# Four more sets of four d_ff blocks by seven block products, in a sparse attention and squared-relu kernel on one core

## The chip, the core and the metric

The kernel runs on one core of one Trainium2 chip. Times are device microseconds of that core. The engines are TensorE (PE in the profile, with its weight loads as PEld), VectorE (DVE), ScalarE (ACT), GpSimd (POOL) and SyncE (SP). POOL and SP issue the transfers between memory and the core's buffers; SP also issues the transposes that are made by a transfer.

## What is computed

The reference is attention with 4 batches of 768 tokens, 8 heads of 64 channels, where a token sees 8 global tokens and the last 96, with a bias that grows with distance; its output, 3072 tokens by 512 channels, goes through two weight matrices with a squared relu between.

```
scores = scale * np.matmul(q, k.transpose(0, 1, 3, 2))
...
keep = is_global | is_local
...
a = np.exp(scores)
a = a / (np.sum(a, axis=-1, keepdims=True) + 1e-09)
...
x = np.ascontiguousarray(attn_out.transpose(0, 2, 1, 3)).reshape(B * S, H * D)
h = np.maximum(x @ w_in, 0.0)            # 3072 x 512 by 512 x 2048
return (h * h @ w_out).astype(np.float32)  # 3072 x 2048 by 2048 x 512
```

## The kernel before

**Halves.** The 3072 tokens are cut into eight halves of a batch (`halves[0]` to `halves[7]`, 384 tokens each). Each half goes through attention (scores, exp on ScalarE, a product with a mask on VectorE, the product with the values, a norm on VectorE), a transpose of the result to `x.xt` (channels on the partitions), layer 1 (`x.xt` by `w_in_sb`, relu, square, to `x.h2`) and layer 2 (`x.h2` by `w_out_sb`, to `y`, stored to memory). While layer 1 of one half runs, the scores and values of the next half and layer 2 of the half before are placed between its products.

**Layer 1 in two ways.** d_ff has 16 blocks of 128 hidden units. `layer1` makes one block plainly: four matmuls of 384 columns into a PSUM bank, then `relu` into `hr` on ScalarE or VectorE (L744, L746), and for each two blocks one `square` (L758, L760). The other way, `layer1_group`, takes four blocks at once: two near ones (2g and 2g + 1) and the two that lie eight blocks further, so that tokens, channels and hidden units form a 2 by 2 by 2 block product. It makes that product of eight block products by seven, as in Winograd's form of Strassen's method: the steps p1 to p7 are four matmuls of 192 columns each (L841), some with plain operands, some with sums of blocks. The sums of `x.xt` stand in `x_mix` (four sums per half, `list_x_mix`, L818). The sums of the weights stand in `in_mix` for the groups 1, 2 and 3 (`list_in_mix`, L785), and for group 0 in columns of `w_in_sb` whose plain weights aren't read any more (`list_late_mix`, L801).

**What a set of seven leaves to the other engines.** A bank of partial sums is copied out by `hold` (the tile `kept`, L256 on ScalarE, L258 on VectorE) three times, and the kept copies are added to later sums by `add`, an operation of VectorE alone (L901), which also takes the relu. In half 2 the sets are *seeded* (`SEEDS`): there one of the three adds is replaced by a copy of `kept` back into a bank (`seed`) and a plain `relu` (L907). Then come two squares (L924, L926).

**Which sets.** The strings of `LAYER1` say which groups of a half go by seven and in which sequence the steps are listed: the seven letters of a group's alphabet in `LETTERS` are its steps, an `s` is one plain block. In the kernel before, half 2 has groups 3 and 2 by seven and eight plain blocks, halves 3 and 4 have groups 3, 2 and 1 by seven and four plain blocks, halves 5, 6 and 7 have all four groups by seven: 20 sets. Halves 0 and 1 are plain.

**The order.** Every operation is first listed, by the stages above, in three lists: the jobs of TensorE (`p` and a number), the loads (`l`), and all the rest. The string `ORDER` then says in which sequence they are issued and on which engine: `a` ScalarE, `d` VectorE, `s` SyncE, `g` GpSimd; the digits behind a point are the PSUM banks that a job opens, `@` names a transfer that a load has to come behind. Each engine works its own words in that sequence. The numbers are places in the lists, so they shift when operations are added ahead of them.

Of the kernel before, what the change touches and what calls it, by code (L numbers as in the profile page):

```python
# [9 lines left out]
FP16 = mybir.dt.float16  # L10
# [3 lines left out]
P = 128  # L14
# [29 lines left out]
LAYER1 = {2: "sasbcsdABCsesDEsFGfsgs", 3: "as123456b7cdsAeBCfgDsEFsG",  # L44
          4: "AasBbCscDEdefF123ss45gG67", 5: "1A2BCDh3E45iF6jabckdlefgGm7n",
# [6 lines left out]
ORDER = """a4 d1 g2 p0.0 a6 s8 d12 a0 s10 d13 l3 l1 a18 l2 d15 d19 a26 d16 d3 l5 a30 d14 a20 a27 d9 l4 a23  # L52
d5 a22 d17 p1.12+31 a21 l0 p5.34 d11 a7 p10.56 l6 a28 p3 a24 l10 a31 d32 l9 a33 p6 d34 p4.7 a39
l7 p11 d37 a29 p9.0 p8.1 a46 l8 p2.23 d43 a40 p19.7 d35 l11 a47 p7 d55 a25 p13.51 d36 l13 a41
d44 p14.4 p12.67 d48 p15 a42 l12 d59 p17 a49 p16.0 p22.2 d45 l14 p24.4 a52 d51 p23.36 a50 d38
p34.50 l16 d58 a53 p21.7 d64 p25.2 a60 l18 p27.1 d65 a57 p20.4 a61 p32.37 d66 a81 d56 p31.2 l15
a73 p29.6 d68 p18.5 d72 p28.4 a74 p26.3 l19 p36.1 d54 a69 p35.2 p30.7 a86 d70 p33.54 d85 a71 d91
p39.16 a67 p40.27 a77 d63 p37.3 a82 d75 l17 a78 d62 p41.5 a92 d79 d76 p38.0 d84 d80 p45.4 d83
l21 a97 p48.1 d96 a101 l20 a98 p44.2 a89 p47.5 d107 l23 p46.7 a112 p42.0 d111 a108 d110 a93
p43.2 d109 p53.1 a87 p52.5 d102 p50.4 p49.7 a113 l22 d120 d100 a90 d105 p59.6 l27 a116 d119 a103  # L60
d106 p55.3 p51.1 l29 d94 a122 a88 d128 p65.2 l28 a104 d95 a117 p64.4 a118 p58.5 a129 a136 d114
p60.0 d99 a137 l30 d146 d191 p54.3 l24 p62.6 d115 d205 l25 p57.1 a133 p56.4 d125 d121 p63.7
p67.6 a123 d134 d135 a130 d206 p61.1 p72.3 a126 d132 p69.4 d189 a124 p77.7 a131 d156 p70.0 a142
p82.1 d157 d165 a159 p71.5 a160 p74.4 d162 l34 a166 d201 a163 p83.6 d147 a161 l26 p73.0 a167
d522 d164 a138 p84.3 l31 d158 d148 a168 a169 p79.52 d186 l35 a139 d202 p89.04 p81.1 d127 a198
l33 d151 p85 a187 d170 a178 d523 p86 a174 d207 a199 d184 p78.06 a179 d149 l32 p80.57 p88.41 d180
p87 a195 l36 d200 a175 p76.2 d203 a185 l37 d155 p75.4 a196 d193 p91.0 l38 a188 d143 s194 d197
p66.1 a181 l39 d172 a171 p95.3 d152 a173 p90.5 d223 p100.4 d153 a209 s224 a176 d236 p92 d204
p103.2 d177 d208 p68.3 d237 s216 a244 a140 d210 p93.6 d240 a211 p94 a182 d150 s217 a144 d219
p96.1 p104 d225 p97 d183 a245 d221 p98.7 s220 d239 a218 p102.3 d238 p111 d214 d228 s226 l44 p106  # L70
d222 d243 l43 d213 p109.61 s229 d227 p110.73 d154 p99 l40@217 a255 d258 s215 d141 p101 a256
l42@217 d145 a251 d272 d190 p113 l45 a252 a234 p114.73 d254 l41@217 d192 p108.61 p105.0 a248 l46
d246 a261 p107 d253 d259 a262 l47 d257 s260 p115.62 a249 s235 d230 p116.74 l48 p118.3 a264 d250
p131.1 a265 d232 d263 p117.6 a268 d231 a292 p122.2 d266 a273 p121.7 d233 a269 d212 p125.1 a271
d280 s324 p124 d284 p127.4 a283 p126 d241 a278 d267 p123.6 d285 a293 p137.1 s325 d281 p119.5
a287 p132 a286 p129.7 a279 d294 p130 p140 d323 a301 p142 d270 p134.6 a290 d274 a307 p128.1 a291
p135 d288 p133.2 a308 p136 d298 p141.5 a310 d300 s242 a299 p143.1 s282 a297 d309 p139 d326 p138
d524 p112 d395 l50@325 a305 s275 d311 p120 a303 l56 d306 a312 s289 d295 a302 p146.36 l53 p147.54
d304 p145.71 a330 s296 d313 l51@325 a333 p144.2 a331 d318 l52 p148.3 a334 d319 a276 l49@325
p149.5 d321 a327 a322 d433 d332 a328 l54 p151.64 p150.07 d314 p152 d320 a338 l57 d329 p159.1  # L80
a339 l55 p157.0 d336 a337 p172.7 a341 d340 p153 a352 d370 a342 p160.3 a350 d315 p169.6 s371 d353
a344 p158.7 p162 d351 p161 p154.4 d316 a355 d397 p166.3 a347 p164.7 d356 p163 s398 p156 d317
d358 d359 a366 p171.1 d343 p165 s399 p167 a360 d362 p181.7 a363 d335 a361 p170 d345 p175 d367
p177 a357 p174.0 d375 p173.5 a378 d373 p178.3 s247 s277 d369 p176 a383 s354 p180 d368 a372
p155.0 d349 a379 p168.1 a376 d382 a384 d400 p179 p183 l58@399 a364 p182.7 d380 a348 p184 s374
a377 l65 d385 p185.3 a389 l62 a387 d381 s386 p188.41 a365 d388 p187.05 l59@399 p186.27 a405
p189.6 d401 a409 l63 a413 d402 p190.0 a406 d416 l73 a410 d403 p191 a407 l61 d396 a414 p193.42
d412 a417 p194.65 l60@399 d411 a418 p192.71 p195 a422 d415 a419 l64 d391 p200.4 d429 a420 p206.7
d437 a426 p198.0 d392 p219.1 s438 d393 a434 d408 a427 p207.6 p204.4 d394 a447 s346 d489 p210
d443 a462 p202.5 a451 d428 p199.1 a423 d404 p211 a441 p213 d435 p197.4 p217.2 a432 d456 p205.5  # L90
s436 p218.1 d424 a444 d452 p196 d480 s491 a445 d476 a461 d460 p203.6 p215.7 d442 p223 a458 p221
d425 a453 p208 d421 s492 p209 d481 p220 a448 d483 p222.1 a469 d477 p214 a446 d467 p227.6 s390
d431 s468 p212.0 d457 p201 d449 a464 d493 a463 p216.1 d454 p224 a484 l70 p225 d459 s455 p230
a439 d473 a471 l66 d465 p226 a496 p231.50 d470 a474 l69@492 s430 p236.13 d478 p233.42 a497 s490
p228.7 d472 a503 l72 d482 a498 p229.5 l67@492 a509 d479 d494 a504 p241.4 l71 p235 a510 d485 d475
a527 d505 p237.01 a495 l68@492 a466 p232.72 d499 p234 l74 a500 d525 d486 a450 p245.3 d506 l75
p240.7 d508 p247 a512 s507 d515 p246.5 a533 p239 d488 a532 d487 d516 a526 p255 a501 p250 d520
p259.0 d544 s521 p249.2 d531 p243.6 d536 p252 a535 p238.3 d529 a540 d517 a513 p253 a549 d502
p261.5 s576 a519 p256 d514 p257.6 p270 d545 p263 d546 p244 a551 s440 a553 d541 a565 p248.1 d511
a530 p268.6 p272 d561 p267 a534 p251.2 d560 p260.4 a566 s562 p262 d537 p269 d550 p258.6 a542  # L100
p266 s547 d548 p242.4 a563 d538 a568 p254.0 a552 s577 d518 p264 a528 p271 a578 d554 p274 d567
d543 p265.7 p273 d579 p275 a580 a555 d569 p279 d558 a564 p281.2 d556 a596 a570 p276.60 a559 d585
s557 d571 p277.54 p278.71 a586 p280 d600 a593 s539 a589 d601 p282.6 a604 d603 a587 p286 a594
d598 d602 a590 p284.75 a605 d588 p283.03 p285.14 a609 p289 d595 a616 a613 s599 d668 p291 s574
a606 d619 d581 a607 p288.7 d572 p290.1 d622 a610 s575 d582 p303.0 a620 d591 p306.3 a639 d612
s573 p294 d608 a618 a643 d611 p323.5 a614 d671 d626 p305.4 p307 d642 p310 a644 p292.6 d584 d621
p295 a623 p321.4 d583 a628 d647 p296 d664 p312 d615 p298 s665 a629 p301 d650 p287.1 d632 p308.3
a617 s627 p297.4 d636 s597 p322 d645 p313.2 a666 d592 p299.6 a651 d631 p314 a648 p293.0 d652
p311.4 d624 p300 p316 d649 p315 a635 s625 p318.0 a633 d669 p302.4 d672 p309 a634 d655 p320 a667
p304 d653 p326 a662 d637 p324.2 d658 s638 a679 p325.7 a663 d646 s659 d640 p317 a678 p319 p335.4  # L110
d670 a654 p343.0 p328 d673 a707 a641 p334.6 d682 p327 d677 a698 d699 a656 p346.2 d674 a660
p349.3 d712 p337.1 a657 p351 d701 p342 a715 p338.2 d683 a661 p341.1 d680 p355 d675 s681 p329.7
d702 a717 s630 a705 d721 a706 p340 d687 p359 p348 d690 p345 d684 p350.2 d728 p339.3 d714 a704
p330 d688 a716 a703 p347 a691 d722 p354 p344 d710 p332 a720 d676 d708 p360 p362 d685 p331.1 a711
d713 a733 d689 p357 d709 p361 p353.3 a694 d686 a731 p366.0 d719 a692 a729 s693 d725 p352.4 a695
p333 a730 d732 p358 d696 p356 a734 d718 p336 d723 a697 d743 a726 p365.5 d746 a727 p363 d747 d744
p377.6 d700 a724 p364 d739 d735 p367.4 d740 a737 s736 d742 s738 d741 p368 a749 d745 d754 p371.3
d758 p373.2 d761 a762 d757 p369 a765 d750 d755 p374.1 d759 d756 d769 p376 d751 p375 d748 d760
p370 s752 a767 d768 a766 p380 d753 p378 d773 p379 d770 s774 p372 d771 s772 p381 a763 p382 d775
# [85 lines left out]
def kernel(  # L205
# [1312 lines left out]
    for hb in range(1, NHB):  # L1518
# [18 lines left out]
        if hb == 1 and GROUPS:  # L1537
            side.append((8 * 0.65, list_in_mix))
# [68 lines left out]
```

## Time and profile before

| | |
|---|---|
| median of 3 runs | 200.19 us (199.85 to 201.06) |
| the profiled execution | 200.43 us |
| its span, first to last instruction | 198.7 us |
| PE busy | 191.6 us, 96% |
| DVE busy | 176.3 us, 89%, 450 instructions |
| ACT busy | 151.0 us, 76%, 321 instructions |
| POOL busy | 66.9 us, 34% |
| granted TensorE clock | 1.000 of full speed |

The profile is of one execution, whose own time is 200.43 us: 1.73 us lie outside the span. An engine is busy from the start to the end of each of its instructions, and instructions that overlap count once. A "group" of the profile is all instructions of one line, engine and kind, with the mean duration of one of them; "idle before" is the idle time of that engine just ahead of them. The chain that ended last is followed back from the last instruction to what released each.

### The profile page before, as it was taken

The page shows a single profiled execution, that of the slowest core. Times are in us where ns is not written, and L with a number is a line of the kernel's source. Part 1 is how long each engine was busy: PE and PEld are TensorE (multiplying, and loading weights), DVE is VectorE, ACT ScalarE, POOL GpSimd, SP SyncE. Part 2 cuts the span into 40 slices and gives each one's busy share as a digit, 9 for nine tenths or more (in the row PEclk, how much of TensorE's full clock was granted, in tenths as well). Part 3 has the DMA queues.
Part 4 walks back from the last instruction along what each step waited for, and adds up shares of the span by engine and source line. Part 5 has one row for each costly group of instructions (what it writes and reads, how often), then busy time and mean ns, then how long its engine had stood idle before and what let it go on. Part 6 is the DMA issues. An engine that isn't in the chain of part 4 may idle for free.

```text
span 198.7 us, 5980 instructions
## 1 busy us (share of the span) xinstructions
PE 191.6 (96%) x2381; PEld 163.2 (82%) x2381; DVE 176.3 (89%) x450; ACT 151.0 (76%) x321; POOL 66.9 (34%) x82
## 2 busy tenths in 40 slices
PE   7798999999999999999999999999999999999993
PEld 3576899856888687788888998999889999999993
DVE  7589696899999999999989999899899996978971
ACT  6799797899555888976999679878897578769211
POOL 8996565187108701940194007800000000000000
PEclk9999999999999999999999999999999999999999
DMA  5999999999999998999899799996531221201214
GB/s 152 182 150 194 189 180 172 209 195 155 182 192 92 155 205 218 107 127 145 218 118 153 104 222 129 161 175 147 102 102 37 94 57 40 109 0 53 109 53 158
DMA packets 106987, 27.52 MB, mean 139 GB/s; under 512 B 97104, under 2 KB 104016, under 8 KB 106960
## 3 DMA queue, kind: packets, MB, share of 16 engines
q0 software_dynamic: 74944, 13.11, 90.1%
q1 hardware_dynamic: 30816, 13.45, 31.7%
q10 hardware_dynamic: 1200, 0.59, 1.1%
q8 instruction: 18, 0.29, 0.6%
q14 instruction: 9, 0.07, 0.1%
HBM read 27.26 MB, written 6.29 MB: 169 GB/s over the span
## 4 chain that ended last, share of the span: by engine, by line
PE 78%; DMA 7%; POOL 5%; DVE 5%; ACT 3%; issue 1%; POOLq 0%; DVEq 0%
PE yps L1064 32%; PE hps L841 19%; PE hps L717 14%; PE sp L610 4%; DMA xt<-tm 4%; DMA w_mix<-in_k_dram 4%; PE av L671 3%; PE yps L978 3%; POOL w_mix L396 2%; POOL v L396 1%; DVE hr L901 1%; ACT h L758 1%; PE av L1380 1%; PE trp L549 1%; DVE vb L258 1%
## 5 line engine op out<-in xcount | busy, mean ns | idle before, releaser
L623 ACT ACTIVATE ex<-sp 128x512 f16<-128x512 f32 x66 | 36.7, 632 | 3.6 <-PE sp L610 3.5
L1064 PEld LDWEIGHTS <-h 128*128 128x128 f16 x376 | 33.9, 98 | 4.0
L717 PE MATMUL hps<-xt,w_in_sb 128*128 128x128 f16 (+2 forms) x288 | 35.6, 273 | 0.3 <-ACT ex L1350 0.3
L256 ACT COPY kept<-hps 128x384 f32<-128x384 f32 x52 | 24.6, 490 | 12.4 <-PE hps L841 8.8
L901 DVE CUSTOM_DVE_ANT_0 hr<-hps,kept 128x384 f16<-128x384 f32 x58 | 30.3, 548 | 1.0 <-PE hps L841 0.6
L717 PEld LDWEIGHTS <-w_in_sb 128*128 128x128 f16 x288 | 23.5, 98 | 5.9 <-DMA w_in_sb<-in_moe_w_in_dram 0.5
L1064 PEld LDWEIGHTS <-mixed 128*128 128x128 f16 x272 | 25.2, 98 | 3.6 <-DVE mixed L1029 0.2
L396 POOL DMA_DIRECT2D sq<-in_q_dram x19 | 17.3, 910 | 31.0 <-DMA q<-sq 23.4
L256 ACT COPY y<-yps 128x256 f32<-128x256 f32 (+2 forms) x39 | 14.6, 385 | 15.8 <-PE yps L1064 15.8
L396 POOL DMA_DIRECT2D sk<-in_k_dram x19 | 17.1, 903 | 24.9 <-DMA q<-sq 22.4
L841 PEld LDWEIGHTS <-w_in_sb 128*128 128x128 f16 x288 | 24.4, 98 | 1.0
L841 PEld LDWEIGHTS <-in_mix 128*128 128x128 f16 x272 | 22.8, 98 | 1.1 <-issue 0.3
L841 PE MATMUL hps<-x_mix,in_mix 128*128 128x192 f16 x204 | 23.4, 246 | 0.0
L1064 PE MATMUL yps<-w_mix,h 128*128 128x256 f16 (+1 forms) x192 | 22.4, 264 | 0.0
L1064 PE MATMUL yps<-w_mix,mixed 128*128 128x256 f16 (+1 forms) x184 | 22.2, 268 | 0.0
L396 POOL DMA_DIRECT2D v<-in_v_dram x24 | 21.8, 922 | 1.2 <-DVE h L760 0.6
L1064 PE MATMUL yps<-w_out_sb,h 128*128 128x256 f16 (+1 forms) x184 | 21.9, 268 | 0.0
L924 ACT ACTIVATE h<-hr 128x768 f16<-128x768 f16 x25 | 20.9, 857 | 0.0
L647 DVE TENSOR_TENSOR phat<-ex,mask 128x1024 f16<-128x1024 f16 (+1 forms) x36 | 20.6, 590 | 0.1
L744 ACT ACTIVATE hr<-hps 128x384 f16<-128x384 f32 (+1 forms) x35 | 18.5, 546 | 2.8 <-PE hps L717 2.8
L841 PE MATMUL hps<-xt,w_in_sb 128*128 128x192 f16 x172 | 19.8, 246 | 0.0
L1126 DVE TENSOR_TENSOR y<-yps,y 128x256 f32<-128x256 f32 (+1 forms) x30 | 11.9, 408 | 3.5 <-PE yps L1064 2.9
(110 smaller groups left out, 354.1 us busy)
## 6 DMA issues: line engine op xcount, KB each, us to landing
out_dram<-y SPq DMA_DIRECT2D x23, 256.0 KB, 2.6
v<-in_v_dram POOLq DMA_DIRECT2D x24, 128.0 KB, 7.1
sq<-in_q_dram POOLq DMA_DIRECT2D x19, 128.0 KB, 6.4
sk<-in_k_dram POOLq DMA_DIRECT2D x19, 128.0 KB, 6.4
w_in_sb<-in_moe_w_in_dram POOLq DMA_DIRECT2D x4, 512.0 KB, 11.0
w_out_sb<-in_moe_w_out_dram POOLq DMA_DIRECT2D x4, 512.0 KB, 12.3
y<-in_q_dram SPq DMA_DIRECT2D x2, 256.0 KB, 4.4
y<-in_k_dram ACTq DMA_DIRECT2D x2, 256.0 KB, 5.1
```

The lines of the kernel that those rows point to most:

```text
L256: nc.scalar.copy(out=out, in_=in_)
L396: dma = nc.gpsimd.dma_start(out=dst, in_=src[x.b, :, r0 + t * P:r0 + (t + 1) * P, :] .rearrange("h p d -> p h d"))
L610: nc.tensor.matmul(sp[h][:, i, :], lhsT=lhsT, rhs=x.q[rows, r % HT, a, :], start=True, stop=True)
L623: nc.scalar.activation(out=st["ex"][:, h], in_=sp[h], func=AF.Exp, scale=scale)
L647: eng(e).tensor_tensor(out=x.phat[a][:, :, t0:t0 + n], op=ALU.mult, in0=st["ex"][:, :, i0:i0 + 2 * n].rearrange("p e (t b) c -> p e t (b c ...
L717: nc.tensor.matmul(st["ps"][:, i * n:(i + 1) * n], lhsT=w_in_sb[:, kk, m * P:(m + 1) * P], rhs=x.xt[:, kk, c0:c1], start=kk == 0, stop=kk ...
L744: nc.scalar.activation(out=o, in_=i, func=AF.Relu)
L841: nc.tensor.matmul(st[name][:, i * HC:(i + 1) * HC], lhsT=left(i, kk), rhs=right(kk), start=fresh and i == kk == 0, stop=kk == KK - 1, ski ...
L901: eng(e)._custom_dve(dve_ops.TENSOR_ADD_SAT, out=hidden(which)[:, :, cols], in0=sums(name), in1=st[kept], s0=3.4e38, s1=0.0)
L924: nc.scalar.activation(out=h2, in_=hr, func=AF.Square)
L1064: nc.tensor.matmul(st[bank_name][:, 0:n], lhsT=a(m), rhs=b(m)[:, cols], start=fresh and m == 0, stop=m == HK - 1, skip_group_check=not fresh)
L1126: eng(e).tensor_tensor(out=y, in0=ps, in1=y, op=ALU.add)
```

## The change

Groups 0 and 1 of half 2, and group 0 of halves 3 and 4, are now made by seven block products instead of four plain blocks each: all 24 sets of halves 2 to 7. The weight sums of `in_mix` are made in two parts, for groups 2 and 3 together and for group 1, and are listed earlier; a product waits for the two chunks of `w_in` that it reads, and not for all four. The sums of group 0 (`list_late_mix`) are listed at half 2, since that is the first half that needs them. `ORDER` is a new string; its loads (`l`) stand in the same sequence as before.

```diff
-LAYER1 = {2: "sasbcsdABCsesDEsFGfsgs", 3: "as123456b7cdsAeBCfgDsEFsG",
-          4: "AasBbCscDEdefF123ss45gG67", 5: "1A2BCDh3E45iF6jabckdlefgGm7n",
+LAYER1 = {2: "abcdABCeDEFGfg1h2i3jk4l567mn", 3: "ah1i23j4k56bl7cmdnAeBCfgDEFG",
+          4: "AahBbiCcjDEdkelfF123mn45gG67", 5: "1A2BCDh3E45iF6jabckdlefgGm7n",
...
-ORDER = """a4 d1 g2 p0.0 a6 s8 d12 a0 s10 d13 l3 l1 a18 l2 d15 d19 a26 d16 d3 l5 a30 d14 a20 a27 d9 l4 a23
...
-s764 s776 a777 a778"""
+ORDER = """a4 d1 g2 s8 p0.0 a0 s10 l3 d12 d13 l1 a6 a18 l2 d15 d19 a26 d16 a30 l5 d3 a20 a27 d14 a23 l4 a22
...
+p390 d791 a795 a796 p384 s792 d788 s790 p393 a781 s782 d793 s794"""
...
-    in_mix, in_mix_ops = [], [[] for _ in range(4)]
+    in_mix, in_mix_ops = [], {g: [] for g in GROUPS}
...
-    def list_in_mix():
-        near = slice(GROUPS[0] * 2 * P, (GROUPS[-1] + 1) * 2 * P)
+    def list_in_mix(groups):
+        near = slice(groups[0] * 2 * P, (groups[-1] + 1) * 2 * P)
         far = slice(near.start + d_ff // 2, near.stop + d_ff // 2)
+        at = slice(near.start - GROUPS[0] * 2 * P, near.stop - GROUPS[0] * 2 * P)
...
-                eng(e).tensor_tensor(out=in_mix[i], in0=a, in1=b,
+                a, b = [in_mix[t][:, :, at] if type(t) is int else t for t in (a, b)]
+                eng(e).tensor_tensor(out=in_mix[i][:, :, at], in0=a, in1=b,
                                      op=ALU.subtract if i else ALU.add)
...
+            sums[i] = plan.add({"DVE": 0.1 + KK * (near.stop - near.start) * 0.00053}, weight_sum,
+                               needs + [w_in_op[groups[0] // 2], w_in_op[2 + groups[0] // 2]])
...
-            needs = needs + (late_mix_ops[0] + late_mix_ops[2] if i == 3 else
-                             in_mix_ops[0] + in_mix_ops[2])
+            mine = in_mix_ops.get(places[i], late_mix_ops)
+            needs = needs + mine[0] + mine[2]
...
-            job = plan.pe(2 * KK * (HC / 2400 + 0.003), emit, needs + [w_in_op[c] for c in range(4)],
-                          int(fresh))
+            job = plan.pe(2 * KK * (HC / 2400 + 0.003), emit,
+                          needs + [w_in_op[g // 2], w_in_op[2 + g // 2]], int(fresh))
...
     list_mix()
+    list_in_mix(GROUPS[1:])
+    list_in_mix(GROUPS[:1])
...
-        if hb == 1 and GROUPS:
-            side.append((8 * 0.65, list_in_mix))
```

More of the change, by code (lines that the diff above doesn't have):

```diff
@@ L57 @@
[L57 to L62, printed above, removed]
@@ L93 @@
[L93 to L98, printed above, removed]
@@ L781, in weight_sum @@
                 if not in_mix:
-                    mix = const.tile([P, 4, KK, near.stop - near.start], FP16, name="in_mix")
+                    mix = const.tile([P, 4, KK, len(GROUPS) * 2 * P], FP16, name="in_mix")
                     in_mix.extend(mix[:, i] for i in range(4))
-                a, b = [in_mix[t] if type(t) is int else t for t in (a, b)]
-                eng(e).tensor_tensor(out=in_mix[i], in0=a, in1=b,
+                a, b = [in_mix[t][:, :, at] if type(t) is int else t for t in (a, b)]
+                eng(e).tensor_tensor(out=in_mix[i][:, :, at], in0=a, in1=b,
                                      op=ALU.subtract if i else ALU.add)
-            needs = [in_mix_ops[t][0] for t in (a, b) if type(t) is int]
-            in_mix_ops[i].append(plan.add(
-                {"DVE": 0.1 + KK * (near.stop - near.start) * 0.00053}, weight_sum, needs + w_in_op,
-                plan.rank + MIX[4]))
+            needs = [sums[t] for t in (a, b) if type(t) is int]
+            sums[i] = plan.add({"DVE": 0.1 + KK * (near.stop - near.start) * 0.00053}, weight_sum,
+                               needs + [w_in_op[groups[0] // 2], w_in_op[2 + groups[0] // 2]])
+            for g in groups:
+                in_mix_ops[g].append([sums[i]])
     def list_late_mix():
@@ L803, in list_late_mix, with x_ready @@
             needs = [late_mix_ops[t][0] for t in (a, b) if type(t) is int] + plain_jobs[places[i]]
-            needs = needs + (late_mix_ops[0] + late_mix_ops[2] if i == 3 else
-                             in_mix_ops[0] + in_mix_ops[2])
+            mine = in_mix_ops.get(places[i], late_mix_ops)
+            needs = needs + mine[0] + mine[2]
             late_mix_ops[i].append(plan.add({"DVE": 0.1 + KK * 2 * P * 0.00053}, late_sum, needs))
+    def x_ready(x, k0, k1):
+        if x.hb > 1:
+            return [x.x_ops[a] for a in range(k0, k1)]
+        return [x.x_ops[a, t] for a in range(k0, k1) for t in range(HT)]
     def list_x_mix(x):
         b = lambda k, n: x.xt[:, k * KK:(k + 1) * KK, n * HC:(n + 1) * HC]
-        first, second = [x.x_ops[a] for a in range(KK)], [x.x_ops[a] for a in range(KK, NCT)]
+        first, second = x_ready(x, 0, KK), x_ready(x, KK, NCT)
         x.t_ops = []
@@ L830, in layer1_group @@
         gs = slice((g - GROUPS[0]) * 2 * P, (g - GROUPS[0] + 1) * 2 * P) if g else None
-        sum_ops = in_mix_ops if g else late_mix_ops
+        sum_ops = in_mix_ops[g] if g else late_mix_ops
         def product(name, fresh, left, right, needs):
@@ L865, in plain @@
             return (lambda kk: x.xt[:, k * KK + kk, n * HC:(n + 1) * HC],
-                    [x.x_ops[a] for a in range(k * KK, (k + 1) * KK)])
+                    x_ready(x, k * KK, (k + 1) * KK))
         def mixed(k):
```

124 lines of the change are left out of this document (69 added, 55 removed).

## The prediction

> **What bounds the kernel now.** I read the page first: the busy table, the slices and the shares of the chain.
>
> ```profile
> PE 191.6 (96%) x2381; PEld 163.2 (82%) x2381; DVE 176.3 (89%) x450; ACT 151.0 (76%) x321; POOL 66.9 (34%) x82
> PE   7798999999999999999999999999999999999993
> DVE  7589696899999999999989999899899996978971
> PEclk9999999999999999999999999999999999999999
> PE 78%; DMA 7%; POOL 5%; DVE 5%; ACT 3%; issue 1%; POOLq 0%; DVEq 0%
> ```
>
> TensorE is full from the fourth slice on, at full granted clock, and 78% of the chain that ended last is TensorE. But VectorE is in its nines as well from 40 us to about 160 us. So the second view is the busy time by stage; a line has the stage, its length, and the busy us of PE, PEld, DVE, ACT and POOL with their instructions.
>
> ```profile
> 20.00:40.00 20.00, 19.93 (x258) 17.80 (x259) 15.93 (x49) 16.69 (x35) 9.59 (x12) 1.00 1.71 188
> 40.00:67.00 27.00, 26.99 (x308) 19.86 (x308) 26.48 (x65) 19.34 (x42) 14.73 (x18) 1.00 1.74 162
> 67.00:81.00 14.00, 14.00 (x180) 10.69 (x176) 13.34 (x37) 12.17 (x27) 3.83 (x5) 1.00 1.59 184
> 81.00:101.00 20.00, 19.72 (x254) 16.83 (x250) 18.96 (x45) 16.27 (x35) 7.73 (x10) 1.00 1.84 150
> 101.00:123.00 22.00, 22.00 (x288) 19.27 (x283) 21.62 (x55) 18.44 (x42) 8.29 (x11) 1.00 1.30 149
> 123.00:165.00 42.00, 42.00 (x543) 38.66 (x541) 39.91 (x91) 33.80 (x71) 5.24 (x6) 1.00 0.80 110
> 165.00:198.70 33.70, 30.63 (x341) 28.65 (x338) 24.08 (x63) 17.87 (x39) 0.00 (x0) 1.00 0.21 74
> ```
>
> The cuts are mine: layer 1 of half 2 lies in 67 to 81, that of half 3 in 81 to 101, that of half 4 in 101 to 123. TensorE idles 0.01 + 0.00 + 0.28 + 0.00 = 0.29 us between 40 and 123 us. VectorE idles 0.52 + 0.66 + 1.04 + 0.38 = 2.60 us there, ScalarE 7.66 + 1.83 + 3.73 + 3.56 = 16.8 us. Third, the chain in order of time (start, us, what) tells where another engine already paces the kernel.
>
> ```profile
> 67.85 1.30 PE hps L717 x8
> 69.15 0.33 PE hps L841 x4
> ...
> 70.78 0.34 PE hps L841 x4
> 71.15 0.29 ACT kept L256
> ...
> 76.55 1.00 DVE hr L901 x2
> ...
> 80.60 0.56 DVE tm L681
> 81.19 7.00 DMA xt<-tm
> 88.28 0.36 DVE x_mix L818
> ...
> 92.85 0.48 DVE kept L258
> 93.38 1.15 PE hps L841 x12
> ```
>
> Up to 70.78 and from 93.38 on the chain is TensorE without a break worth naming. Between them, in layer 1 of half 2 and the first of half 3, it runs through copies on ScalarE, adds and norms on VectorE and the transposes of half 3, although TensorE lost only 0.28 us there. So the kernel is bound by TensorE's work, with no slack on VectorE for 22 us in the middle, which is where the change puts half of its work.
>
> **The change, part by part.** *TensorE.* A plain set is four blocks of four matmuls of 384 columns, 16 matmuls; from 67.85, eight of them take 1.30 us, so a set takes 2.60 us. A set by seven is 28 matmuls of 192 columns; from 69.15, four take 0.33 us, so it takes 2.31 us. A set saves 0.29 us, four save 1.16 us. In rows: L717 loses 64 matmuls, L841 gains 112. Weight loads follow the count of matmuls and run beside them (PEld is 82% busy); 69.15 shows four products with their loads hidden. All this lies on the path that sets the end, as TensorE has no idle time in these stages.
>
> *Copies and adds.* These rows have the prices (line, kind, count, busy us, mean ns, idle before):
>
> ```profile
> L901 DVE CUSTOM_DVE_ANT_0 hr<-hps,kept 128x384 f16<-128x384 f32 x58 | 30.3, 548 | 1.0 <-PE hps L841 0.6
> L256 ACT COPY kept<-hps 128x384 f32<-128x384 f32 x52 | 24.6, 490 | 12.4 <-PE hps L841 8.8 <-DVE hr L901 3.1 <-DVE mixed L1029 0.3
> L744 ACT ACTIVATE hr<-hps 128x384 f16<-128x384 f32 (+1 forms) x35 | 18.5, 546 | 2.8 <-PE hps L717 2.8
> L924 ACT ACTIVATE h<-hr 128x768 f16<-128x768 f16 x25 | 20.9, 857 | 0.0
> L926 DVE TENSOR_TENSOR h<-hr 128x768 f16<-128x768 f16 x15 | 8.2, 549 | 1.5 <-ACT hr L907 1.1 <-PE yps L1064 0.5
> L785 DVE TENSOR_TENSOR in_mix<-w_in_sb 128x1536 f16<-128x1536 f16 x2 | 1.9, 954 | 0.3 <-DMA w_in_sb<-in_moe_w_in_dram 0.3
> L801 DVE TENSOR_TENSOR w_in_sb<-w_in_sb 128x512 f16<-128x512 f16 x4 | 1.7, 417 | 0.0
> L488 DVE TENSOR_TENSOR w_mix<-w_out_sb 128x1024 f16<-128x1024 f16 x4 | 2.7, 685 | 0.0
> ```
>
> A plain set has four relus and two squares, 6 operations. A seeded set (half 2) has three holds, a seed, two adds, two relus and two squares, 10; the others have three holds, three adds, a relu and two squares, 9. So the four sets add 4 + 4 + 3 + 3 = 14 operations of 0.49 to 0.55 us; back to back on VectorE two adds take 1.00 (76.55), so 0.50 us each, and 14 take 7.0 us of the two engines. A relu may go on either engine, an add only on VectorE: 16 relus become 6, and 10 adds come. The weight sums in two parts cost 685 + 417 ns in place of 954, 0.15 us more for each of four sums, 0.6 us, and four more instructions, all on VectorE. Together 18 operations.
>
> *Which engine.* I counted the words of ORDER: 320 `a` and 392 `d` before, 313 and 417 after. So the 18 and 7 more go to VectorE. Up to the first layer 1 jobs of half 5 (p240 before, p252 after, near 123 us) there are 218 `a` and 253 `d` before, 222 and 268 after: 15 more on VectorE and 4 more on ScalarE by then. The other ten `d` come later, where VectorE idles 2.1 and 9.6 us; they leave ScalarE and are free.
>
> *What covers this.* Up to 123 us, VectorE gets 11 operations at 0.50 us besides the four halved sums at 0.6 us, 6.1 us, into stages where it is 80.40 us busy of 83.00 and which are to shrink by 1.16 us: 86.5 of 81.84, an excess of 4.7 us. Busy time can be packed tighter, though. An add takes 0.548 us alone and 0.50 when another follows at once, so each of the 65 + 37 + 45 + 55 = 202 instructions in these stages that isn't followed at once now could give 0.05 us. If half of them stand loose, that is 5 us, and the excess is covered. So the bounds of this term are 0 and 4.7 us. I take it as nearly covered, because the additional operations are holds, seeds and squares in large part, whose readers come many products later; only the adds free a bank at once. What a late add delays is a PSUM bank, and with it the next product that opens one.
>
> *A rule on this point.* VectorE's stages above are 95 to 98% busy while ScalarE has 16.8 us to spare. The Trainium skill (Perfetto Trace Analysis, Optimizing Scalar/DVE Operations) says that work which either engine can do may be moved to Scalar when DVE is saturated; the change moves it the other way, 7 operations from ScalarE to VectorE. By that rule the time would be the second rival's below, not the sum's.
>
> *Earlier due times.* Half 2 needs the sums of groups 1 and 0, which before served half 3 and half 5. The late sums' line (count, durations, first and last start):
>
> ```profile
> L801 DVE TENSOR_TENSOR w_in_sb<-w_in_sb x4: 417/417/418, 40.5 to 124.6; 128x512 f16<-128x512 f16 x4
> ```
>
> The last of them must now come before about 80 us, 0.42 us more in the full stretch (it is in the 15 words). The sums of `x_mix` are made for each of halves 2 to 7 already, so none is added. The wait for two chunks of `w_in` in place of four changes nothing: layer 1 of halves 0 and 1 has read all of `w_in` before the first product by seven.
>
> *Queues.* No transfer is added, and the 76 loads stand in the same sequence, so POOL's queue is as before. SP's stores and transposes keep their number; the transposes of half 3 sit on the chain at 81.19 and wait on a norm of VectorE, so that norm is the one that a fuller VectorE must not delay. The first 42 jobs of TensorE stand in the same sequence, so the opening, where the loads pace, costs nothing.
>
> *New stalls.* With the plain blocks gone from half 2, eight jobs of 0.65 us that waited for no copy are gone from between the steps of the sets. The view of waits has, for TensorE within this stretch, just one row:
>
> ```profile
> PE av L671 <- DVE phat L647: 0.2, 1, 0.2
> ```
>
> The new stalls lie between none and the 4.7 us above; nearest to this row, I take 0.4 us, as one copy (0.49 us) that comes late.
>
> *Sum.* Against the profiled execution: 200.43 - 1.16 + 0.4 = 199.67 us. That execution lies 0.24 us above the median of the runs, so I forecast **199.4 us**; its own range is 199.0 (no new stall, 200.19 - 1.16) to 200.0.
>
> **The rivals.** *First, the sets of half 2 wait for their own copies: no change, 200.1 us.* The step c of a set needs the bank of a copied out, 0.49 us after a's last matmul; with only b (0.33 us) between, TensorE stands for the rest, and plain blocks no longer fill in. One late add of 0.55 us in each of the two new sets of half 2 is 1.1 us: 200.19 - 1.16 + 1.1. For it speaks that the chain already runs through copies and adds from 71 to 93 us; against it that TensorE lost only 0.28 us there, because scores, values and layer 2 of other halves lie between.
>
> *Second, VectorE becomes the bound between 40 and 123 us: slower, 201.4 us.* The place is its full stages, the price the excess: if half of the 4.7 us can be packed away, 200.19 - 1.16 + 2.35 = 201.4; if none, 203.7. It decides once less than 3.5 us of the excess fits, as 4.7 - 3.5 is the saving. For it speaks VectorE's 2.60 us of idle time against 6.1 us of new work; against it the looseness of busy time, and 16.8 us of ScalarE, four more words of which are used.
>
> *Third, better than the sum, 198.8 us:* the parted weight sums and the new order take away waits that now cost the 0.28 us as well. TensorE is full at the rate of its rows everywhere else from 20 us on, so hardly more than 0.3 us beyond the saving can be had.
>
> **How the numbers follow.** The likeliest (199.0 to 200.0) gets 0.48, the first rival (200.0 to 200.6) 0.20, the second (200.6 to 203.7) 0.28, the third (below 199.0) 0.04. The range of 198.8 to 202.2 leaves out the upper half of the second rival's times and half of the third's, about 0.15. Within 1% of 200.19, which is about what a measurement of this kernel can tell from no change, is 198.2 to 202.2. Faster than that would need more than TensorE's work gives, 0.04; slower is the second rival with two thirds or more of its price unpacked, 0.13; the rest is 0.83.
>
> **What would show it.** In the profile after: L717 with 224 matmuls and L841 with 672; PE busy about 190.5 us; adds x68 for x58; VectorE near 475 instructions and 184 us busy. If the sum is right, TensorE still idles less than 0.7 us between 40 and 123 us. If the first rival is, PE waits for `kept` or `hr` of ScalarE or VectorE appear between 67 and 81 us. If the second is, TensorE's waits lie on VectorE through all stages to 123 us, the chain there is mostly VectorE, and ScalarE idles beside it. A time under 198.8 would mean that TensorE had waits hidden in its busy time, and one above 203.7 a transfer that comes late, which I see no cause for; either would make the working wrong.

## The result, and the profile after

The changed kernel takes 207.07 us (median of 4 runs, 206.57 to 208.96) against 200.02 us (199.68 to 201.06, 4 runs) on the same chip: a ratio of 1.036, interval 1.029 to 1.044. It is 7 us slower; the forecast was 199.4 us and the range ended at 202.2. (Medians and ratios leave out disturbed executions, and the ratios are taken over the runs, so some differ a little from the quotient of the medians.)

The execution in the profile is the slowest of the four, 208.96 us with a span of 207.1; the one before took 200.43 with 198.7. Its busy table, slices and chain:

```profile
PE 193.8 (94%) x2429; PEld 167.5 (81%) x2429; DVE 185.8 (90%) x474; ACT 147.6 (71%) x315; POOL 66.7 (32%) x82
PE   6788999999997999599999998999999999999993
DVE  7599899999995999579999999999999999978882
PEclk9999999999999999889999999999999999999999
PE 49%; DMA 17%; DVE 14%; POOL 9%; ACT 4%; SPq 4%; issue 3%; POOLq 0%
```

The counts are the predicted ones (L718 has 224 matmuls, L850 672, adds are 68, VectorE has 474 instructions), so the change does what it says. But TensorE has dips at slices 13 and 17, a lower clock in slices 17 and 18, and only half of the chain. The stages, cut as before:

```profile
20.00:40.00 20.00, 19.49 (x254) 17.37 (x255) 18.97 (x57) 14.79 (x31) 11.12 (x14) 1.00 1.71 187
40.00:67.00 27.00, 25.87 (x298) 19.53 (x296) 24.06 (x61) 20.93 (x49) 12.44 (x15) 1.00 1.88 158
67.00:81.00 14.00, 13.33 (x187) 11.57 (x188) 13.57 (x35) 11.09 (x24) 2.89 (x4) 1.00 1.85 193
81.00:101.00 20.00, 17.86 (x200) 15.30 (x198) 16.49 (x39) 16.10 (x34) 8.02 (x10) 0.91 1.87 144
101.00:123.00 22.00, 21.77 (x303) 19.89 (x301) 21.50 (x54) 17.22 (x37) 7.01 (x8) 1.00 1.07 125
```

TensorE idles 1.13 + 0.67 + 2.14 + 0.23 = 4.17 us from 40 to 123 us, where it idled 0.29 before; over the whole span 207.1 - 193.8 = 13.3 us against 198.7 - 191.6 = 7.1. So 6.2 of the 8.4 us of span are idle time: 3.9 of them from 40 to 123 us, 0.8 before and 1.5 after. The other 2.2 are busy time, though 1.16 us of work was to be saved; 1.7 of these 3.4 us are a stretch at half clock, shown below, and the rest isn't settled by any row. The half clock isn't what makes the kernel slower: the mean clock was 0.992 in two of the four executions (208.96 and 206.99 us) and 1.000 in the other two (206.57 and 207.16). VectorE was *less* busy in 40 to 67 (24.06, before 26.48) and in 81 to 101 (16.49, before 18.96): it waited too. The waits (us in all, times, longest):

```profile
DVE x_mix L827 <- DMA xt<-tm: 4.0, 2, 2.4
PE hps L850 <- DMA xt<-tm: 2.1, 1, 2.1
PE av L672 <- DVE phat L648: 1.4, 2, 0.8
PE sp L611 <- DMA q<-sq: 0.9, 2, 0.7
PE hps L850 <- ACT kept L257: 0.5, 1, 0.5
```

All but the last go back to transposes: of `xt`, and of the queries (here 0.7 of the 0.9 us lie at 126 us). The third does so through VectorE's queue, as its timeline shows (start, us, what, idle before):

```profile
62.62 0.34 DVE L827 TENSOR_TENSOR x_mix<-xt 128x384 f16<-128x384 f16 x1
65.34 0.36 DVE L827 TENSOR_TENSOR x_mix<-xt 128x384 f16<-128x384 f16 x1 [2.38 <-DMA xt<-tm]
65.61 0.35 DVE L827 TENSOR_TENSOR x_mix<-xt,x_mix 128x384 f16<-128x384 f16 x1
65.88 0.42 DVE L648 TENSOR_TENSOR phat<-ex,mask 128x512 f16<-128x512 f16 x1
...
66.69 0.68 DVE L648 TENSOR_TENSOR phat<-ex,mask 128x1024 f16<-128x1024 f16 x1
```

The `x_mix` sums of half 2 stand in ORDER ahead of two weighings of scores of half 3. The weighings need no transpose, but they stand behind instructions that do, and TensorE's product with the values waits for both. In the old kernel the first of these sums came behind evictions and weighings, and VectorE didn't wait there:

```profile
66.14 0.41 DVE L258 COPY y<-yps 128x256 f32<-128x256 f32 x1
66.47 0.67 DVE L647 TENSOR_TENSOR phat<-ex,mask 128x1024 f16<-128x1024 f16 x1
67.23 0.36 DVE L818 TENSOR_TENSOR x_mix<-xt 128x384 f16<-128x384 f16 x1
```

At 83 us TensorE itself does the same: the first product of half 3 that needs all four transposes holds everything behind it.

```profile
82.50 0.82 PE L850 MATMUL hps<-xt,w_in_sb 128*128 128x192 f16 x8
85.46 0.50 PE L850 MATMUL hps<-xt,w_in_sb 128*128 128x192 f16 x4 [2.14 <-DMA xt<-tm]
...
86.00:87.00 1.00, 1.00 (x13) 0.77 (x12) 0.66 (x2) 0.57 (x2) 1.00 (x2) 0.53 2.58 153
...
88.00:89.00 1.00, 1.00 (x17) 0.70 (x17) 1.00 (x3) 0.78 (x2) 0.14 (x1) 0.50 3.48 148
...
90.00:91.00 1.00, 1.00 (x12) 0.84 (x11) 0.15 (x1) 1.00 (x4) 0.00 (x0) 1.00 3.72 141
```

(The last three are one-us stretches; the third number from the right is the granted clock.) Behind the hole the clock is 0.5 for 3.4 us, which costs this execution another 1.7. The transposes themselves aren't later than before: the last of half 3 landed at 85.42, and before at 88.19. What moved is the reader. The new order brings TensorE to the waiting product at 83.3; the old one had scores, values and layer 2 ahead of it, and came to such a product with the second four of these eight matmuls:

```profile
87.94 0.82 PE L841 MATMUL hps<-xt,w_in_sb 128*128 128x192 f16 x8
```

### The profile page after: what moved, and what is told of

Its sections match the earlier page's. It is cut to its first block, busy times and chain, and to the rows that moved or that the text cites. A ratio compares the mean times of both kernels' runs of the same rounds, so it can differ in the third digit from the quotient of the medians.

```text
span 207.1 us, 6085 instructions
## 1 busy us (share of the span) xinstructions
PE 193.8 (94%) x2429; PEld 167.5 (81%) x2429; DVE 185.8 (90%) x474; ACT 147.6 (71%) x315; POOL 66.7 (32%) x82
## 4 chain that ended last, share of the span: by engine, by line
PE 49%; DMA 17%; DVE 14%; POOL 9%; ACT 4%; SPq 4%; issue 3%; POOLq 0%
PE yps L1073 21%; PE hps L850 15%; DMA v<-in_v_dram 9%; PE hps L718 6%; DMA q<-sq 6%; PE sp L611 3%; DVE phat L648 3%; POOL w_mix L397 3%; DMA xt<-tm 2%; POOL v L397 2%; SPq L568 2%; DVE hr L910 2%; POOL sq L397 2%; POOL sk L397 2%; ACT h L933 2%
## 5 line engine op out<-in xcount | busy, mean ns | idle before, releaser
L910 DVE CUSTOM_DVE_ANT_0 hr<-hps,kept 128x384 f16<-128x384 f32 x68 | 36.2, 549 | 3.5 <-PE hps L850 2.2
L850 PEld LDWEIGHTS <-w_in_sb 128*128 128x128 f16 x384 | 32.3, 98 | 4.8 <-DMA xt<-tm 2.4
L257 ACT COPY kept<-hps 128x384 f32<-128x384 f32 x58 | 27.1, 486 | 11.4 <-PE hps L850 4.1
L850 PE MATMUL hps<-xt,w_in_sb 128*128 128x192 f16 x216 | 25.7, 248 | 2.1 <-DMA xt<-tm 2.1
L850 PEld LDWEIGHTS <-in_mix 128*128 128x128 f16 x288 | 24.9, 99 | 1.1 <-issue 0.7
L850 PE MATMUL hps<-x_mix,in_mix 128*128 128x192 f16 x216 | 25.2, 250 | 0.0
L933 ACT ACTIVATE h<-hr 128x768 f16<-128x768 f16 x28 | 23.9, 857 | 0.1
L718 PE MATMUL hps<-xt,w_in_sb 128*128 128x128 f16 (+2 forms) x224 | 23.0, 257 | 0.2 <-DMA w_in_sb<-in_moe_w_in_dram 0.2
L718 PEld LDWEIGHTS <-w_in_sb 128*128 128x128 f16 x224 | 17.6, 98 | 3.4 <-DMA w_in_sb<-in_moe_w_in_dram 0.4
L850 PE MATMUL hps<-x_mix,w_in_sb 128*128 128x192 f16 x168 | 19.1, 246 | 0.2 <-DVE hr L910 0.2
L916 ACT ACTIVATE hr<-hps 128x384 f16<-128x384 f32 x25 | 12.4, 505 | 3.9 <-PE hps L850 3.7
```

The source lines that it names most:

```text
L257: nc.scalar.copy(out=out, in_=in_)
L718: nc.tensor.matmul(st["ps"][:, i * n:(i + 1) * n], lhsT=w_in_sb[:, kk, m * P:(m + 1) * P], rhs=x.xt[:, kk, c0:c1], start=kk == 0, stop=kk ...
L850: nc.tensor.matmul(st[name][:, i * HC:(i + 1) * HC], lhsT=left(i, kk), rhs=right(kk), start=fresh and i == kk == 0, stop=kk == KK - 1, ski ...
L910: eng(e)._custom_dve(dve_ops.TENSOR_ADD_SAT, out=hidden(which)[:, :, cols], in0=sums(name), in1=st[kept], s0=3.4e38, s1=0.0)
L916: nc.scalar.activation(out=o, in_=i, func=AF.Relu)
L933: nc.scalar.activation(out=h2, in_=hr, func=AF.Square)
```

## The experiments

Theory A: the places that the new ORDER gives to the steps cost the time. Rivals: B, VectorE is the bound from 40 to 123 us (the prediction's second rival); C, the sets wait for their own copies (its first); D, the added sets cost it, whatever the order.

**Fewer packets, and less on VectorE.** In both kernels the q and k loads of halves 2 to 7 took whole rows of 2 KB (the rows' places are then others than the reference's).

```diff
-  dma = nc.gpsimd.dma_start(out=dst, in_=src[x.b, :, r0 + t * P:r0 + (t + 1) * P, :].rearrange("h p d -> p h d"))
+  whole = src.rearrange("b h s d -> (b h s) d")[n0:n0 + P * H, :]
+  dma = nc.gpsimd.dma_start(out=dst, in_=whole.rearrange("(p h) d -> p h d", h=H))
```

> The changed kernel, with the 36 loads of q and k of halves 2 to 7 reading the same number of bytes as whole rows of 2 KB in place of pieces of 256 B; the tokens then stand in another sequence, so q and k of those halves are other values. Theory A (the new order puts the x_mix sums, the products and the scores of halves 2 to 4 too close behind transfers, and VectorE and TensorE, which work in order, stand until these land): the loads and the transposes behind them land earlier, and the waits of the profile on q<-sq and xt<-tm (2.1 + 0.9 us on TensorE, 4.0 us on VectorE) go: 203.5 us or less. Theory B (VectorE has too much work between 40 and 123 us): 206.5 to 207.5 us, as its work is the same. Theory C (the sets wait for their own copies): as B.

> The kernel before with the same loads of q and k as whole rows (values of q and k of halves 2 to 7 are other ones). Theory A: TensorE waits for no transfer there, so 199.5 to 200.3 us, within 0.5 us of before. If it falls by over 1 us as well, transfers pace the kernel before too, and a fall of the changed kernel by as much says nothing of the order.

Measured: 205.14 us (two runs; ratio 1.025, 1.019 to 1.031) and 202.41 us (1.012, 1.008 to 1.016). The loss shrank by 2 us only, less than A had said, and the old kernel became slower although its packets fell from 106,987 to 74,732. TensorE waited for transposes of `xt` there for 0.5 and 0.3 us, which it doesn't in the old kernel: its order seems fitted closely to when things land. Then eleven holds, relus and squares of the new kernel went from VectorE to ScalarE:

```diff
-d275 ... d238 ... d286 ... d293 ... d312 ... d313 ... d326 ... d386 ... d506 ... d471 ... d517
+a275 ... a238 ... a286 ... a293 ... a312 ... a313 ... a326 ... a386 ... a506 ... a471 ... a517
```

> The changed kernel, with 11 operations between the first layer 2 pair and half 5 (8 holds, 2 relus, 1 hand-out) moved from VectorE to ScalarE at the same places of the order: VectorE has some 5 us less to do there. Theory B: 202 to 205 us. Theory A and theory C: 206.3 to 207.5 us, as neither a transfer nor the sequence changes.

Measured: 208.45 us (two runs; 1.042, 1.035 to 1.049). Nothing gained: B falls, as the stages had said. Last, the new kernel with an ORDER sought anew over the steps' listed costs:

```diff
-ORDER = """a4 d1 g2 s8 p0.0 a0 s10 l3 ...
+ORDER = """(the same 1268 steps in another order, some on the other engine)
```

> The changed kernel with all its 24 sets, its two-part weight sums and every operation, but another ORDER: the same words moved, with other engines for some, so that sums and products stand further behind the transfers they wait for. Theory A: 198.5 to 200.5 us, that is the 1.16 us of TensorE's work and no more than 1.5 us of waits. Theory B: 203 us or more, since VectorE's work is within 3 us of what it is. Theory C: 202 us or more, since the sets are the same.

Measured: 206.72 and 208.53 us (1.038, 1.030 to 1.045). A's number fell with it. In the profiled execution, of 210.70 us, TensorE again waited for transposes of `xt`, 3.2 us, and in the opening, which the search had also reordered, 2.5 us for a copy.

**The order against the work.** To part the two I carried one kernel's order over to the other's work: words of steps that both have keep their sequence on each engine; the steps that one lacks were fitted in (or plain blocks put back), with the `x_mix`, late and weight sums; PSUM banks behind the opening were given out anew. Two more kernels had their later order sought anew.

```diff
-LAYER1 = {2: "sasbcsdABCsesDEsFGfsgs", ...    ORDER of the old kernel
+LAYER1 = {2: "abcdABCeDEFGfg1h2i3jk4l567mn", ...    same order, 28 products for 16 blocks   (sets24_old_order)
-LAYER1 = {2: "abcdABCeDEFGfg1h2i3jk4l567mn", ...    ORDER of the new kernel
+LAYER1 = {2: "sasbcsdABCsesDEsFGfsgs", ...    same order, 16 blocks for 28 products   (sets20_new_order)
```

> The new kernel's work, all 24 sets and the weight sums in two parts, in the old kernel's ORDER: every word that both kernels have stands in the old sequence, with the old queue of loads, turns, transposes and stores and the old opening; only the words of the four new sets, the two-part weight sums, the late sums and the x_mix sums were fitted in. Theory A (it is the places that the new ORDER gives to the common steps) expects 199 to 202 us, near the old kernel. Theory D (it is the added sets themselves: their x_mix sums and first products need the transposes of halves 2 and 3 early, whatever the order around them) expects 205 to 208 us.

> The converse: the old kernel's work, 20 sets with four plain sets, but in the new kernel's ORDER, with the plain blocks put where the four sets stood and everything else in the new sequence, the new queue on SP among it. Theory A expects 203 to 207 us, although nothing of the added sets is in it. Theory D expects 200 to 201 us, as the old kernel.

> All 24 sets from the order of the first kernel of this call, with every step after the opening free to move, and the transposes and turns on SP issued early enough for landings 2 us later than planned. If sets by seven products are worth what their product count says (1.16 us) once the order leaves room for late transposes, 198 to 200.5 us, and under the fourth kernel of this call by about 1 us. If the sets cost more than they save whatever the order, over 201 us.

> The old kernel's 20 sets, its opening kept, its later order sought anew in the same way as the third kernel's: the control of that search. 199 to 201 us expected; the difference from the third kernel, about 1 us in that one's favour by the product count, is what the four sets are worth in orders found alike.

| | old order | new order | sought anew |
|---|---|---|---|
| 20 sets | 200.2 | 209.15 (1.046, 1.039 to 1.054) | 206.68 (1.029, 1.021 to 1.036) |
| 24 sets | 206.18 (1.027, 1.022 to 1.032) | 207.07 (1.036, 1.029 to 1.044) | 207.75 (1.035, 1.030 to 1.041) |

The old work in the new order is slowest of all: the order alone costs 9 us, so A holds in this corner (2.7 of these are idle time from 20 to 40 us, where the new kernel itself idles 0.5). The sets in the old order cost 6 us, as D has it. The old order fits only the old work, and 24 sets take 206.2 to 207.8 us in all three. The control, the old work in an order sought anew, lost 6.5 us as well, so the search can't tell what four sets are worth. TensorE's waits with 24 sets in the old order lie in VectorE's queue:

```profile
PE hps L851 <- DVE tm L683: 1.8, 1, 1.8
...
PE hps L851 <- DVE y L1136: 0.9, 1, 0.9
...
PE hps L851 <- DVE hr L911: 0.8, 1, 0.8
PE hps L851 <- DVE kept L260: 0.7, 1, 0.7
```

That doesn't show D, though. The `x_mix` sums had to be fitted into the old order as well, and the two longest of these waits stand behind such sums, which themselves waited for transposes; here a norm behind a sum of half 3:

```profile
90.74 0.36 DVE L828 TENSOR_TENSOR x_mix<-xt,x_mix 128x384 f16<-128x384 f16 x1 [2.33 <-DMA xt<-tm]
...
91.24 0.56 DVE L683 TENSOR_TENSOR tm<-av,rec 128x384 f16<-128x384 f32 x1
```

The last two rows, 1.5 us on `hr` and `kept`, are the sets' own adds and copies, as C has it.

**Are the transfers late?** Four kernels loaded an eighth of the token data (one head of eight) of `q` and `k` from half 2 on and of `v` from half 4 on, and two left out the token loads of halves 4 to 7; both compute something else, with the steps in the same places.

```diff
-  dma = nc.gpsimd.dma_start(out=dst, in_=src[x.b, :, ...])
+  nh = H if x.hb < 2 or name == "v" and x.hb < 4 else 1
+  dma = nc.gpsimd.dma_start(out=dst[:, 0:nh], in_=src[x.b, 0:nh, ...])     (light)
+  if x.hb > 3: return None                                                (no loads)
```

> The old kernel with an eighth of the token data: of k and q of halves 2 to 7 and of v of halves 4 to 7 only one head of eight is loaded (same instructions, same waits, same order; the other heads keep the rows of the halves before, so that part of the computation is changed). It is the measure for the next kernels. By its waits the old kernel loses 0.3 us to transposes, so 198.5 to 200.2 us under every theory.

> The new kernel with the same eighth of the token data. Theory T (the waits come from transposes and turns that land late among the token loads: 2.1 us on transposes of half 3, 2.4 us on VectorE for those of half 2, 0.9 us on queries) expects them gone: 198 to 201 us, no more than 1 us over the light old kernel, or under it by up to the 1.2 us that the four sets save. Theory O (the new places of the steps make the engines wait for each other, whatever the transfers) expects 204 to 207 us, 4 us or more over the light old kernel.

> All 24 sets fitted into the old order, with the same eighth of the token data. Its waits in full were on VectorE's norm of half 3 (1.8 us), on copies and sums of the new sets (1.9 us) and 0.9 us on an eviction. Theory T expects 199 to 202 us, some 4 us less than its 206.2. Theory O expects 204 to 206.5 us, since those waits name VectorE and ScalarE.

> The old 20 sets in the new order, with the same eighth of the token data; in full it took 209.2 us, with 2.7 us lost at 30 to 35 us and 2.2 us at 67 to 70 us. Theory T expects 200 to 204 us, Theory O 206 to 209 us. What is lost before 40 us lies ahead of the lightened loads and should stay under both.

> The old kernel without the token loads of halves 4 to 7 (k, q and v of these halves are left out; the turns and everything after them work on the rows of halves 2 and 3). The transposes of halves 3 and later then have the queues to themselves but for turns and stores. It is the measure of the next kernel: 198 to 199.5 us under both theories, as it waited for transposes for 0.3 us only.

> The new kernel without the token loads of halves 4 to 7. Theory X (a transpose that is issued among token loads, however small, lands 3 to 7 us after its issue, not 1.2, and the new order has its first products of half 3 and its x_mix sums of half 2 too close behind) expects the two waits of 1.8 and 0.6 us that were left with an eighth of the data to go: 201 to 203 us. Theory O (engines wait for each other in the new order, whatever the transposes) expects 204 to 205.5 us, as with an eighth of the data.

Measured, light: old 199.41 us (0.995, 0.993 to 0.997), new 205.30 (1.024, 1.020 to 1.028), 24 sets in the old order 202.44 (1.009, 1.006 to 1.012), 20 sets in the new order 206.50 (1.029, 1.026 to 1.033). No loads: old 200.03 (0.997, 0.995 to 1.000), new 205.14 (1.021, 1.015 to 1.027). Against the old kernel with the same loads, the new one still loses 5.9 us (light) and 5.1 us (no loads) of its 7, so the bytes are 1.2 us of the loss and the loads of halves 4 to 7 altogether 1.9. The expectations of T and X, that their lateness is the whole, fall, and O's ranges hold for the new order. With 24 sets in the old order, which came out between T and O, 3.0 of 6.0 us are left. The holes of the new kernel shrink and stay at the same places, here without the loads:

```profile
PE av L682 <- DVE phat L658: 1.1, 2, 0.8
PE hps L860 <- DMA xt<-tm: 0.6, 1, 0.6
```

**Parts of the change in the old order.** One kernel has only the weight sums in two parts, the next also the set of half 4 by seven products.

```diff
-    list_in_mix()
+    list_in_mix(GROUPS[1:])
+    list_in_mix(GROUPS[:1])                              (two_part_sums)
-          4: "AasBbCscDEdefF123ss45gG67"
+          4: "AahBbiCcjDEdkelfF123mn45gG67"              (one_set_more)
```

> The old kernel's 20 sets and its old order on TensorE, ScalarE, SP and GpSimd word for word; of the change only the weight sums in two parts, and the places of VectorE's weight sums, late sums and x_mix sums fitted anew. The four added instructions take some 0.2 us more in all. If the sums' split costs nothing, 199.5 to 201 us; over 202 us it would be part of the loss.

> As the kernel before in this call, and of the four sets only that of half 4 (its first group, late in VectorE's fuller stretch) by seven products; the orders of ScalarE, SP and GpSimd as in the old kernel, on TensorE the seven steps where the four blocks stood. By the product count 0.29 us less than the kernel before in this call. If a set pays where its steps find room: 199.2 to 200.8 us. If a set costs by its waits, as four did by 6 us in the old order: 201 to 202.5 us.

Measured: 202.10 us (1.006, 1.003 to 1.009) and 206.70 (1.030, 1.025 to 1.035). The sums alone cost 1.4 us against the old kernel of the same chip (200.72), and one set in half 4 seemed to cost 4.6 more. The timelines of VectorE and TensorE, and a stretch of the clock, say where, and it isn't in half 4:

```profile
63.29 0.75 DVE L761 TENSOR_TENSOR h<-hr 128x512 f16<-128x512 f16 x2
67.19 0.36 DVE L827 TENSOR_TENSOR x_mix<-xt 128x384 f16<-128x384 f16 x1 [3.15 <-DMA xt<-tm]
...
68.54 0.42 DVE L1135 TENSOR_TENSOR y<-yps,y 128x256 f32<-128x256 f32 x1
...
69.81 0.42 DVE L259 COPY y<-yps 128x256 f32<-128x256 f32 x1
...
69.01 0.21 PE L611 MATMUL sp<-q,k 64*128 64x128 f16 x1 [0.97 <-DVE y L1135]
70.28 0.21 PE L611 MATMUL sp<-q,k 64*128 64x128 f16 x1 [0.87 <-DVE y L259]
...
72.00:73.00 1.00, 1.00 (x5) 0.49 (x4) 0.96 (x4) 1.00 (x3) 0.00 (x0) 0.50 1.32 276
```

Fitting in the sums had put the first `x_mix` sum of half 2 ahead of the evictions. VectorE sits 3.15 us on the transposes, the evictions come late, TensorE waits twice for their banks, and the clock halves. All four executions have this half clock (mean clock 0.990 to 0.992). It is the new kernel's pattern in the old order. The run with the two-part sums alone has it in small: VectorE waits 1.7 us for the same transposes ahead of evictions, and TensorE 0.9 us behind them.

**Only the places.** So the last two kernels moved nothing but such places.

```diff
 (one_set_more, VectorE: the four x_mix sums of half 2 behind weighings, as in the old kernel)
-... d234 d276 d158 d258 d250 d162 d236 d257 d263 d261 ... d254 ... d267 d270 d235 d237
+... d276 d158 d258 d250 d162 d257 d263 d261 d234 ... d254 d236 ... d267 d235 d270 d237
 (new kernel, half 2 on VectorE; half 3 on TensorE and VectorE)
-d234 d236 d235 ... d258 ... d261
+d234 ... d258 ... d261 d236 d235
-p160.2 d339 p165.4 a366 l49@341 d337 p152.76 d336 p148 ... d326 ... p119 d325
+p160.2 d339 p152.76 p148 p119 d326 d325 p165.4 a366 l49@341 d337 d336
```

> As the old order with one set more (206.7 us), but VectorE's four x_mix sums of half 2 back in the old kernel's places, each behind a weighing of half 3's scores. Theory P expects the 3.7 us lost at 67 to 75 us (two waits for evictions of 1.1 and 1.0 us, then 3.4 us at half clock) to go, and 202 to 203.5 us. If the added set itself holds the time, 205.5 to 207 us.

> The new kernel with two places of its ORDER changed and no work added or left out. On TensorE the first product of half 3 that needs all four transposes stands behind three jobs that were ready (eight scores, the last product of half 2, four matmuls of the second layer), with VectorE's steps for them ahead of the x_mix sums. On VectorE two x_mix sums of half 2 stand behind the two weighings that TensorE waited for. Theory P (places: what stands in order behind a step that waits for a transpose) expects the hole of 2.1 us at 83 us down to 0.5, the two of 0.8 us at 66 us gone and no stretch of half clock behind the hole (3.4 us at half speed, 1.7 us lost): 202.5 to 205.5 us. If the time is held by something else (later turns, the sets), 206.5 to 208 us, the waits coming back later.

Measured: 202.48 us (1.012, 1.006 to 1.018) with one set more. The places of four instructions gave back 4.2 of the 4.6 us (3.6 by the ratios, as the old kernel took 199.91 us beside this run and 200.72 beside the other), 1.7 of it the half clock. So P's range holds here, and VectorE's timeline shows how: a wait for the same transposes, but with the evictions ahead of it.

```profile
64.91 0.42 DVE L1135 TENSOR_TENSOR y<-yps,y 128x256 f32<-128x256 f32 x1
...
65.92 0.41 DVE L259 COPY y<-yps 128x256 f32<-128x256 f32 x1
...
68.31 0.36 DVE L827 TENSOR_TENSOR x_mix<-xt 128x384 f16<-128x384 f16 x1 [1.38 <-DMA xt<-tm]
```

That is still above the kernel with the sums alone, so this set hasn't been seen to save time.

The new kernel stayed at 207.24 us (1.033, 1.027 to 1.039), so P's range was missed there. Its hole of 2.1 us at 83 us did go, as did both at 66 us (one of 0.5 us for values, `vb`, came in their place), but TensorE then stood at 78 us before scores of half 4, for their queries, and in the profiled execution, the slowest of five with 208.98 us, the half clock followed that hole:

```profile
PE sp L612 <- DMA q<-sq: 3.3, 2, 2.5
...
82.00:83.00 1.00, 1.00 (x6) 0.61 (x5) 0.77 (x2) 1.00 (x3) 1.00 (x2) 0.50 0.65 92
```

Why the queries are late is seen on SP, first in the old kernel, then with the two places moved:

```profile
70.75 1.62 SPq L567 DMA_TRANSPOSE k<-sk  x1
72.56 3.31 SPq L567 DMA_TRANSPOSE q<-sq  x1
75.98 0.52 SPq L1149 DMA_DIRECT2D out_dram<-y  x1
76.61 5.75 SPq L696 DMA_TRANSPOSE xt<-tm  x4
```

```profile
70.92 1.29 SPq L569 DMA_TRANSPOSE k<-sk  x1
72.30 2.04 SPq L1159 DMA_DIRECT2D out_dram<-y  x1
74.51 3.49 SPq L569 DMA_TRANSPOSE q<-sq  x1
78.10 3.81 SPq L698 DMA_TRANSPOSE xt<-tm  x3
```

The new order has a store between the turn of the keys and that of the queries, which starts 1.95 us later than in the old kernel. The queries landed at 80.47 us (before 77.94; in the new kernel, where the store stands at the same place, 79.62). While TensorE lost time at 66 us, it waited for them only 0.25 us; with those holes smaller it waited 2.5. Moving that store wasn't tried. So in the new kernel it is shown that these places hold the waits, and that curing two lets the next hold the time; how the 7 us split over all of them stays open, and so does whether 24 sets in a better order would beat 200 us. None of the kernels run here with the whole data did.

## Why the prediction was wrong

*TensorE's saving*, 1.16 us, was counted rightly in matmuls, but no run shows it. With light loads and at a mean clock of 0.999 to 1.000, TensorE was busy 192.2 us (new order) and 191.8 (old order) with 24 sets, and 191.3 with 20; the forecast was a fall from 191.6 to about 190.5. Where the saving went isn't settled by any row.

*New stalls* is the term that failed. It was 0.4 us with bounds of 0 and 4.7. TensorE's idle time rose by 6.2 us in the profiled execution, which had 1.7 us of half clock on top. Its upper bound was taken from VectorE's work, and the waits don't come from work: VectorE idled more, not less (7.4 us from 40 to 123 us, before 2.6).

*Queues* is the step behind it. It counted what SP and POOL issue and found the counts unchanged. But ORDER is also the sequence of each engine, and the change finds the later orders anew. A store came ahead of the turn of the queries, `x_mix` sums ahead of weighings, products of half 3 ahead of ready scores. I had read that the transposes of half 3 take 7.0 us and cost 0.28, and took the 0.28 as a property of the kernel; it was one of its order, which had other work ahead of their first reader. The clause "that norm is the one that a fuller VectorE must not delay" named the wrong end: the last transpose of half 3 landed earlier than before, and its readers came earlier still.

*Which engine* and *what covers this*: the words were counted rightly, and the cover was no issue. The rule weighed there, of the Trainium skill (Perfetto Trace Analysis, Optimizing Scalar/DVE Operations), to move work to Scalar when DVE is saturated, had no effect here: eleven operations moved gave 208.45 us against 207.07, intervals overlapping.

*The parted weight sums*, 0.15 us each: 202.10 us with them and fitted places in the old order, 1.4 us more, of which their 0.6 us can be a part; the rest may be the places, with the 0.9 us of waits named above, and the banks, which the run doesn't part.

*The rivals.* The first, sets of half 2 that wait for their own copies, has no row there in the new kernel; the one row on `kept`, 0.5 us, lies at 181 us. The second is refuted. What happened was in the last sentence, a transfer that comes late "which I see no cause for"; more exactly, its reader came early. *The opening, at nothing*: TensorE idles 0.84 us more up to 40 us. Behind 123 us, where the prediction called the operations moved to VectorE free, it idles 1.5 us more; no run settles whether they are the cause.

## What to carry to other kernels

When a change finds an order anew, a small wait in the old profile is no sign of slack: for each transfer that takes long, compare the place of its first reader in both orders, and list what stands behind that reader on its engine without needing the transfer. Put the ready work of an in-order engine ahead of the step that may wait; the places of four instructions were worth 3.6 to 4.2 us, at least three times the whole saving that was forecast. And look for all such holes before judging a cure, since here one that was taken away uncovered the next.

## What the runs showed of the hardware

A hole in TensorE's work can cost more than its length. In the profiled executions, behind waits of 2.1 us (new kernel), 1.9 (eleven operations on ScalarE), 2.5 (two places) and two of about 1 us close together (one set more) the granted clock was 0.50 for 3.4 us; behind one of 1.8 us (24 sets in the old order) it stayed 1.00. The same program can fall on either side: the mean clock of the new kernel was 0.992 in two executions and 1.000 in two. The Trainium skill (TensorE: Matmul & The Clock Gate, Part 1: The HAM clock gate) gives the half clock and a window of about 3.4 us, and the length agrees; it has the clock fall after at least one idle window of that length, and here holes of about 2 us were enough.

In the new kernel, transposes of `xt` with no token load in the air landed 1.1 to 1.5 us after their issue ended (one took 2.8), and most of those beside loads 3.0 to 4.8 us; with an eighth of the bytes the last of half 3 still took 3.4. And loads with 30% fewer packets made the old kernel 1.2% slower.
